# Rows loaded once, rows back from the eleventh unit, and outputs copied by ScalarE, in a fused mLSTM and feed-forward kernel

## The chip, the cores and the metric

The kernel runs on one core of a Trainium2 chip. A core has TensorE (PE, with its weight loads as a row of their own, PEld), VectorE (DVE), ScalarE (ACT), GpSimd (POOL) and SyncE (SP), which work through their own queues of instructions and wait for one another by semaphores. SP here issues nearly all DMAs, ACT the stores of the result. The metric is the device time of one execution in microseconds (us); lower is better. Everything is float32.

## The reference

Two stages. An mLSTM cell runs over 768 tokens for 4 batches of 8 heads with 40 values each; then a multiplicative feed-forward works on the 3072 x 320 rows that come out.

```
# for every batch, head and token t
m_new = max(f + m, i);  fs = exp(f + m - m_new);  is = exp(i - m_new)
C = fs * C + is * outer(v, k)         # 40 x 40
n = fs * n + is * k
h = C @ q;   denom = max(|n . q|, 1)
y[t] = sigmoid(o_gate) * h / denom
# x = y as (3072, 320)
out = ((x @ w1) * (x @ w2)) @ w3 @ w_out   # 320->1024, 1024->1024, 1024->320
```

The kernel computes the cell in chunks of 64 tokens (a score matrix within the chunk and a state carried between chunks) and multiplies w3 by w_out first, into the tile `w3o`.

## The kernel before

**Units and steps.** A unit n is 128 tokens of one batch with its 8 heads (n = chunk * 4 + batch; 24 units). One loop (from L820) runs 32 steps. Step s makes the outputs of unit s-1 and the scores and state update of unit s (`quarter_work`, L338), and between them the feed-forward of units that are done: `up`, `up_rest` for token groups 0 to 2 (four units each), and from step 19 groups 3 to 5 by a scheme of seven products (`up_by_seven`: `single`, `shared`, `left`, `product`), which needs sums of weights (`weight_sums`, POOL, steps 16 and 17) and sums of tokens (`token_sums`, DVE, steps 17, 21 and 25). `ffn_out` multiplies by `w3o`; ACT copies the result (L741) and stores it.

**Order.** TensorE's instructions are chained one behind another by `in_order`. Each engine works in the order in which the program issues to it; an instruction that waits holds up all behind it on its engine. `tc.issue_after` places a stretch of instructions behind a given one. All of SP's DMAs form one such queue.

**A unit's way.** `load` brings k, v (and q for n < 10) as rows of tokens, `load_o` the output gate, `load_u` rows of U (from n = 10; before that `rows_of_u` makes them by a DVE transpose, L295). `turn` makes kT and qT: for n < 10 by PE transposes (L95) and ACT copies (L325), from n = 10 by one DVE transpose each (L317), from rows that `load_turned` put into two halves of `gates` and `q_all`. For each of k and q and each of the two heads of a pair it issues two DMAs of 32 partitions x 640 values: one in place, one to the next 32 partitions and 32 columns to the left (so that the DVE transpose of 32 x 32 blocks finds values 32 to 39 of each token's 40 there). `weights` are eight exps on ACT (L303), `masks` two selects on POOL (L308), `weighted` and `decayed` multiplies on POOL (L330, L335).

**Outputs.** `outputs` (L419) multiplies the part that comes from the state by the gate (L423, from the bank `cell[1]` in PSUM to `h`), adds the part from the chunk in four quarters (L430, from the same bank), and then takes five operations to y: absolute value (L438), maximum and doubling (L440), reciprocal (L441), output gate (L443), product (L445). The last are spread between the scores' multiply (L397) and the state updates (L404, L414).

**y's way to x.** The feed-forward needs y transposed. For n < 15 (`NY`), `twice` doubles y's last 64 columns on POOL (L476), `x_trans` makes three PE transposes (px, L95) and one ACT copy (L486). From n = 15, `send` (issued at the top of step n+2) writes y to DRAM by four DMAs in pieces of 128 bytes (L456, L458), `get_back` (in the same step, behind the other loads) reads it by four DMAs in pieces of 384 bytes (L465), and `x_turn` is one DVE transpose (L472), which stands ahead of `turn(s + 1)` and `token_sums` on DVE. `load_turned(s + 2)` is issued at the end of a step.

**The third step.** Weights come as raw words (`fetch`), are scaled on ACT (L191) and converted on DVE (L199, L200) in `convert`. In step 2, `between` (L892) puts these, two x_trans and a `warm` between outputs and scores. `warm` issues products of the identity that nobody reads (fill, L92): there one of 128 x 512 and 38 of 64 x 64.

Of the kernel before, what the change touches and what calls it, by code (L numbers as in the profile page):

```python
# [16 lines left out]
def kernel(  # L17
# [29 lines left out]
    L = 64  # L47
# [49 lines left out]
    def warm(n, m=4, small=0):  # L97
        bank = mps([P, 4, P], "fill")
        for _ in range(n):
            mm(bank[:, 0:m], ident, ident.unsqueeze(1).to_broadcast([P, m, P]))  # L100
        for i in range(small):
            r = halves[i % 2]
            mm(bank[r, 0, 0:L], ident[r, 0:L], ident[r, 0:L])
# [8 lines left out]
    N_DIAG = 2  # L112
# [13 lines left out]
    NY = 15  # L126
    KC = KF + 1
    y_d = [dram.tile([P, 4, KC, 32], FP, name=f"y_d{n}") if n >= NY else None for n in range(NU)]
# [12 lines left out]
    def load_turned(n):  # L141
        c, b = divmod(n, B)
        for dst, src in zip(turned_in[n % 2], (k, q)):
            for hip in range(2):
                of = src[b].rearrange("(p two) s d -> two p s d", two=2)[hip, :, c * P:(c + 1) * P, :]
                for j in range(2):
                    p0, c0 = hip * DP + j * 32, (1 - j) * 32
                    nc.sync.dma_start(out=dst[p0:p0 + 32, c0:c0 + NP * RAW].rearrange("r (p e) -> r p e", p=NP),  # L148
                                      in_=of.rearrange("p (r f) d -> r p (f d)", f=4))
# [269 lines left out]
    def outputs(n, pi, ph):  # L419
        c, b = divmod(n, B)  # L420
        hs = slice(b * H, (b + 1) * H)
        h = sb.tile([P, H, D1], FP, name="h", tag="h")
        nc.vector.tensor_tensor(out=h.rearrange("p (n two) d -> p two n d", two=2), in0=pi,  # L423
                                in1=gT[:, c, hs].rearrange("p (n two) -> p two n", two=2).unsqueeze(3)
                                .to_broadcast([P, 2, NP, D1]), op=OP.mult)
        if n < N_DIAG:
            nc.vector.tensor_tensor(out=h, in0=ph, in1=h, op=OP.add)
        for x, e in quarters if n >= N_DIAG else ():
            part = h[halves[x], 0:H // 2] if x == e else h[halves[x], H // 2:H]
            nc.vector.tensor_tensor(out=part, in0=ph[x][halves[e]], in1=part, op=OP.add)  # L430

        den = sb.tile([P, H, 1], FP, name="den", tag="den")

        def steps():
            V = nc.vector
            yield V.tensor_scalar(out=den.bitcast(U32), in0=h[:, :, D:D1].bitcast(U32), scalar1=0x7FFFFFFF, scalar2=None,  # L438
                            op0=OP.bitwise_and)
            yield V.tensor_scalar(out=den, in0=den, scalar1=1.0, scalar2=2.0, op0=OP.max, op1=OP.mult)  # L440
            yield V.reciprocal(out=den, in_=den)  # L441
            e = o_t.pop(n)
            nc.vector.scalar_tensor_tensor(out=e, in0=e, scalar=1.0, in1=den.to_broadcast([P, H, D]), op0=OP.add, op1=OP.mult)  # L443
            y_t[n] = sb.tile([P, DM + REM], FP, name="y", tag="y")
            yield nc.vector.tensor_tensor(out=y_t[n][:, 0:DM].rearrange("p (h d) -> p h d", d=D), in0=h[:, :, 0:D],  # L445
                                           in1=e, op=OP.mult)

        done = steps()
        return lambda: next(done)

    def send(n):


        y = y_t.pop(n)
        for cc in range(KF):
            nc.sync.dma_start(out=y_d[n][:, :, cc, :], in_=y[:, cc * P:(cc + 1) * P].rearrange("t (i c) -> t i c", c=32))  # L456
        for i in range(0, 4, 2):
            nc.sync.dma_start(out=y_d[n][:, i:i + 2, KF, :], in_=y[:, KF * P:DM].rearrange("t (i c) -> t i c", c=32))  # L458
# [3 lines left out]
    def get_back(n):  # L462
        back_t[n] = sb.tile([P, 4, KC, 32], FP, name="yb", tag="yb", bufs=1)
        for i in range(4):
            nc.sync.dma_start(out=back_t[n][32 * i:32 * (i + 1)].rearrange("r m k c -> r m (k c)"),  # L465
                              in_=y_d[n][:, i].rearrange("(m r) k c -> r m (k c)", r=32))

    def x_turn(n):
# [3 lines left out]
        nc.vector.transpose(out=x_t[gr][:, :, j * P:(j + 1) * P].rearrange("c k (m r) -> c k m r", r=32),  # L472
# [60 lines left out]
    for i in range(NBV):  # L533
        nc.gpsimd.memset(vbuf[i][:, :, D:D1], 1.0)
# [3 lines left out]
    nc.gpsimd.memset(gates[RG:P, NP * RAW:TB], 0.0)  # L538
# [281 lines left out]
    for s in range(len(n_up)):  # L820
        if NY <= s - 2 < NU:
            send(s - 2)
# [22 lines left out]
        if s == 2 or N_DVE < s < NY + 2:  # L845
            twice(s - 2)
# [45 lines left out]
        def between():  # L892
            twice(1)
            weighted(2)
            rows_of_u(3)
            for _ in range(3):
                scale_next()
            for n in range(2):
                x_trans(n)
                if n == 0:  # L900
                    warm(1, small=38)
            for _ in range(3):
                convert()
            turn(2)
# [13 lines left out]
        with tc.issue_after(gated.ins) if gated else nullcontext():  # L918
# [11 lines left out]
            if N_DVE <= s + 1 < NU:  # L930
                gated = turn(s + 1)
# [32 lines left out]
        if s == B:  # L964
            for i, r in enumerate(third):
# [5 lines left out]
        if s >= ahead:  # L971
            while pend and len(scaled) < 2:
                scale_next()
        if N_DVE <= s + 2 < NU:
# [37 lines left out]
```

## Time and profile before

| what | value |
|---|---|
| median of 3 runs | 426.45 us (424.92, 426.45, 426.75) |
| span of the profiled execution | 425.8 us, mean granted TensorE clock 0.996 |
| TensorE busy | 414.1 us, 97% |
| VectorE, ScalarE, POOL busy | 74%, 35%, 36% |
| moved by DMA | 51.15 MB, 135211 packets |
| k and q rows of the units from 10 | 112 DMAs of 80 KB, 2.3 to 2.6 us to landing |
| y out and back | 36 DMAs of 64 or 32 KB, 36 of 48 KB |

The profiled execution's own time is its span of 425.8 us. A row of a group gives the line, the engine, the operation, output and input, shapes and count, then busy time and the mean duration in ns, then the idle time before these instructions and what ended it. A row of the timeline gives start and duration in us, then the same, with idle time and releaser in brackets. Where a releaser stands there, the engine waited for it.

### The profile page before, as it was taken

Reading aid. Unit: us, or ns where it says so; the run is one execution under the profiler, and the core shown is the slowest. Engines: PE = TensorE matmul, PEld = TensorE weight load, DVE = VectorE, ACT = ScalarE, POOL = GpSimd, SP = SyncE. Lnnn points to the kernel's source line nnn. Section 1 sums busy time; section 2 is a strip of 40 time slices with the busy share of each in tenths; the row PEclk is TensorE's granted clock in tenths of the full one; section 3 lists DMA queues with packets and bytes.
Section 4 is the critical chain, followed back from the end, with each engine's and each line's share of the span. In section 5 each row is a group of like instructions: output and inputs, shape, how many; then the busy total and the mean of one; then the engine's idle time right before and its main releaser. Section 6 shows DMA issues by size and latency. Waiting matters only on the chain.

```text
span 425.8 us, 13079 instructions
## 1 busy us (share of the span) xinstructions
PE 414.1 (97%) x5353; PEld 335.3 (79%) x5353; DVE 313.5 (74%) x635; ACT 150.1 (35%) x404; POOL 154.3 (36%) x211
## 2 busy tenths in 40 slices
PE   7989989999999999999999999999999999999996
PEld 4768878888688788787777778788778879888896
DVE  6676986888949779778736966596868699575971
ACT  4766865567723623630433313032311110210000
POOL 4421342233303303303307751546453587542100
PEclk9989999999999999999999999999999999999999
DMA  8999998598977776985425675756421120000001
GB/s 186 204 173 245 214 144 140 134 193 180 215 183 154 166 182 135 181 164 105 89 80 130 153 141 121 142 133 117 87 44 36 35 39 2 31 2 31 2 32 62
DMA packets 135211, 51.15 MB, mean 120 GB/s; under 512 B 109360, under 2 KB 126960, under 8 KB 135152
## 3 DMA queue, kind: packets, MB, share of 16 engines
q1 hardware_dynamic: 131552, 46.29, 53.9%
q10 hardware_dynamic: 3600, 4.03, 2.7%
q8 instruction: 42, 0.69, 0.7%
q14 instruction: 17, 0.14, 0.1%
HBM read 44.50 MB, written 5.80 MB: 118 GB/s over the span
## 4 chain that ended last, share of the span: by engine, by line
PE 53%; issue 20%; DVE 7%; POOL 7%; SPq 7%; DMA 5%; ACT 1%; POOLq 0%; DVEq 0%
PE cell L92 17%; PE pa L92 12%; PE o L92 8%; PE pb L92 8%; PE p L92 3%; POOL pw L308 3%; SPq L184 3%; DVE w3T L666 2%; PE pt L95 1%; POOL vw L330 1%; SPq L148 1%; DMA raw<-in_moe_w_dram 1%; PE fill L92 1%; POOL raw L659 1%; POOL state L335 1%
## 5 line engine op out<-in xcount | busy, mean ns | idle before, releaser
L335 POOL TENSOR_TENSOR state<-state,decay 128x164 f32<-128x164 f32 x40 | 20.0, 500 | 154.8 <-DVE state L404 129.0
L92 PE MATMUL pa<-xT,w 128*128 128x256 f32 x240 | 60.4, 382 | 0.0
L92 PEld LDWEIGHTS pa<-xT,w 128*128 128x128 f32 x240 | 44.4, 190 | 6.8 <-DVE h L430 0.4
L303 ACT ACTIVATE pw<-pw,aT 128x64 f32<-128x64 f32 x184 | 46.4, 339 | 3.2 <-ACT o_sb L741 1.9
L92 PE MATMUL pb<-xT,w 128*128 128x256 f32 x192 | 45.4, 379 | 0.0
L729 POOL TENSOR_TENSOR ab<-ab,a_sb 128x512 f32<-128x512 f32 x22 | 29.4, 1356 | 32.2 <-DVE ab L684 32.2
L92 PEld LDWEIGHTS pb<-xT,w 128*128 128x128 f32 x192 | 36.4, 190 | 5.0
L711 POOL TENSOR_TENSOR wo<-wo 128x512 f32<-128x512 f32 x22 | 27.4, 1268 | 29.8 <-DVE wo L686 29.8
L92 PE MATMUL pa<-xT,wr 64*64 64x256 f32 x384 | 37.0, 386 | 0.5 <-DVE wr L200 0.5
L92 PE MATMUL wp<-wo,w3T 128*128 128x320 f32 x128 | 35.9, 433 | 1.1 <-DVE ab L639 0.6
L308 POOL TENSOR_SCALAR_AFFINE_SELECT pw<-pw 64x512 f32<-64x512 f32 x48 | 35.8, 746 | 3.0 <-ACT pw L303 1.2
L92 PE MATMUL pb<-xT,wr 64*64 64x256 f32 x384 | 36.4, 380 | 0.0
L92 PE MATMUL cell<-w3o,ab 128*128 128x320 f32 x128 | 35.4, 432 | 0.0
L638 ACT ACTIVATE a_sb<-pa 128x512 f32<-128x512 f32 x24 | 14.3, 598 | 59.0 <-PE pb L92 59.0
L639 DVE TENSOR_TENSOR ab<-pb,a_sb 128x512 f32<-128x512 f32 x24 | 16.4, 688 | 23.2 <-ACT a_sb L638 22.8
L92 PEld LDWEIGHTS wp<-wo,w3T 128*128 128x128 f32 x128 | 23.8, 190 | 10.5 <-DVE ab L639 0.8
L92 PEld LDWEIGHTS cell<-w3o,ab 128*128 128x128 f32 x128 | 24.3, 190 | 9.5
L92 PEld LDWEIGHTS pa<-xT,wr 64*64 64x64 f32 x384 | 18.9, 132 | 15.4 <-issue 8.8
L686 DVE SCALAR_TENSOR_TENSOR a_sb<-pa,wo 128x512 f32<-128x512 f32 x12 | 8.3, 689 | 29.8 <-PE pa L92 29.8
L430 DVE TENSOR_TENSOR h<-cell,h 64x164 f32<-64x164 f32 x88 | 28.6, 326 | 1.6
L92 PE MATMUL po<-w3o,ab 128*128 128x320 f32 x96 | 26.4, 433 | 0.0
L92 PEld LDWEIGHTS po<-w3o,ab 128*128 128x128 f32 x96 | 18.1, 190 | 7.3
(180 smaller groups left out, 846.4 us busy)
## 6 DMA issues: line engine op xcount, KB each, us to landing
raw<-in_moe_w_dram SPq DMA_DIRECT2D x64, 128.0 KB, 3.4
kbuf<-in_k_dram SPq DMA_DIRECT2D x24, 160.0 KB, 4.5
v_all<-in_v_dram SPq DMA_DIRECT2D x24, 160.0 KB, 4.9
o_in<-in_o_gate_dram SPq DMA_DIRECT2D x24, 160.0 KB, 4.8
pw<-U_d SPq DMA_DIRECT2D x28, 128.0 KB, 3.5
raw<-in_moe_w_dram SPq DMA_DIRECT2D x5, 512.0 KB, 6.7
raw<-in_moe_w_out_dram SPq DMA_DIRECT2D x8, 320.0 KB, 4.1
gates<-in_k_dram SPq DMA_DIRECT2D x28, 80.0 KB, 2.5
```

The source lines that it names most:

```text
L92: in_order(nc.tensor.matmul(out, lhsT=lhsT, rhs=rhs, start=start, stop=stop))
L184: nc.sync.dma_start(out=dst, in_=src)
L303: nc.scalar.activation(out=pw[:, h, :], in_=src[:, h, :], func=AF.Exp, bias=aT[:, c, b * H + h:b * H + h + 1])
L308: nc.gpsimd.affine_select(out=pw[r], in_=pw[r], compare_op=OP.is_ge, fill=0.0, base=0, pattern=[[0, H], [1, L]], channel_multiplier=-1)
L335: nc.gpsimd.tensor_tensor(out=new, in0=old, op=OP.mult, in1=decay[:, b * NP:(b + 1) * NP, 2 * c + x:2 * c + x + 1] .to_broadcast([P, NP, D1]))
L430: nc.vector.tensor_tensor(out=part, in0=ph[x][halves[e]], in1=part, op=OP.add)
L638: nc.scalar.mul(out=a_sb, in_=pa, mul=UP ** -2)
L639: nc.vector.tensor_tensor(out=ab_t[gr][j][:, fs[0]:fs[-1] + 1, t0:t0 + a_sb.shape[-1]], in0=pb, in1=a_sb, op=OP.mult)
L666: nc.vector.tensor_tensor(out=dst, in0=p, in1=q, op=OP.subtract)
L686: nc.vector.scalar_tensor_tensor(out=out, in0=p, scalar=UP ** -2, in1=q, op0=OP.mult, op1=OP.add)
L711: aside_by.tensor_tensor(out=kept[j][:, 1:4:2], in0=kept[j][:, 1:3], in1=kept[j][:, 3:4].to_broadcast([128, 2, TH]), op=OP.add)
L729: aside_by.tensor_tensor(out=t[:, f:FO:FH, :], in0=t[:, f:FO:FH, :], in1=a, op=OP.mult)
```

## The change

- `load_turned` issues one DMA where it issued two, in place. The new `shift` makes the second copy on ACT: four copies of 32 partitions x 16 x 8 values per unit, ahead of `turn(s + 1)` and in ACT's queue ahead of the next unit's exps. A larger part of `gates` is set to zero by POOL in step 4.
- `NY` is 10: units 10 to 14 also go by `send`, `get_back` and `x_turn`.
- `send` is one DMA of whole rows of 384 values (1536 bytes), which include the doubled columns, so `twice` comes ahead of it for every unit; `get_back` is still four DMAs, now in pieces of 128 bytes.
- `twice(s - 1)` and `send(s - 1)` are issued at the end of step s, on SP ahead of `load_turned(s + 2)`; on POOL behind the masks of unit s+1 and in steps 16 and 17 behind `weight_sums`.
- From unit 10 (`N_OWN`), four ACT copies of 64 x 164 bring the chunk's part from PSUM to `h`, behind the multiply by the gate, and one DVE add of 128 x 328 joins the two, in place of four DVE adds.
- The way from `h` to y is four operations: reciprocal, product with -1 and maximum (its absolute value), minimum with one half and product with h, output gate. V's column of ones holds 2.0.
- In the third step, the U rows of unit 3 come behind the three converts, and the fill is two products of 128 x 512.

```diff
--- before.py
+++ after.py
@@ -94,13 +94,10 @@
     def transpose(out, in_, n=P):
         in_order(nc.tensor.transpose(out, in_, ident[0:n, 0:n]))
 
-    def warm(n, m=4, small=0):
+    def warm(n, m=4):
         bank = mps([P, 4, P], "fill")
         for _ in range(n):
             mm(bank[:, 0:m], ident, ident.unsqueeze(1).to_broadcast([P, m, P]))
-        for i in range(small):
-            r = halves[i % 2]
-            mm(bank[r, 0, 0:L], ident[r, 0:L], ident[r, 0:L])
 
     halves = [slice(0, L), slice(L, P)]
     heads = [slice(0, D), slice(DP, DP + D)]
@@ -109,7 +106,7 @@
 
     NB, NBQ, NBV = 4, 3, 5
     N_DVE = N_U = 10
-    N_DIAG = 2
+    N_DIAG, N_OWN = 2, 10
     q_all = const.tile([P, NBQ * H * DP], FP, name="q_all")
     qbuf = [q_all[:, i * H * DP:(i + 1) * H * DP].rearrange("p (h d) -> p h d", d=DP) for i in range(NBQ)]
     kbuf = [const.tile([P, H, DP], FP, name=f"kbuf{i}") for i in range(NB)]
@@ -123,9 +120,9 @@
     decay = const.tile([P, B * NP, NT], FP, name="decay")
     UT = const.tile([P, 2, 3, BH], FP, name="UT")
     U_d = dram.tile([NT, BH, L], FP, name="U_d")
-    NY = 15
+    NY = 10
     KC = KF + 1
-    y_d = [dram.tile([P, 4, KC, 32], FP, name=f"y_d{n}") if n >= NY else None for n in range(NU)]
+    y_d = [dram.tile([P, KC * P], FP, name=f"y_d{n}") if n >= NY else None for n in range(NU)]
 
     o_t, u_t = {}, {}
 
@@ -143,10 +140,15 @@
         for dst, src in zip(turned_in[n % 2], (k, q)):
             for hip in range(2):
                 of = src[b].rearrange("(p two) s d -> two p s d", two=2)[hip, :, c * P:(c + 1) * P, :]
-                for j in range(2):
-                    p0, c0 = hip * DP + j * 32, (1 - j) * 32
-                    nc.sync.dma_start(out=dst[p0:p0 + 32, c0:c0 + NP * RAW].rearrange("r (p e) -> r p e", p=NP),
-                                      in_=of.rearrange("p (r f) d -> r p (f d)", f=4))
+                nc.sync.dma_start(out=dst[hip * DP:hip * DP + 32, 32:TB].rearrange("r (p e) -> r p e", p=NP),
+                                  in_=of.rearrange("p (r f) d -> r p (f d)", f=4))
+
+    def shift(n):
+
+        for mem in turned_in[n % 2]:
+            e = mem[:, 32:TB].rearrange("r (g d) -> r g d", d=D)
+            for p0 in (0, DP):
+                nc.scalar.copy(out=e[p0 + 32:p0 + 64, :, 0:D - 32], in_=e[p0:p0 + 32, :, 32:D])
 
     def load_o(n):
         o_t[n] = io.tile([P, H, D], FP, name="o_in", tag="o_in", bufs=5)
@@ -420,12 +422,18 @@
         c, b = divmod(n, B)
         hs = slice(b * H, (b + 1) * H)
         h = sb.tile([P, H, D1], FP, name="h", tag="h")
-        nc.vector.tensor_tensor(out=h.rearrange("p (n two) d -> p two n d", two=2), in0=pi,
+        y = y_t[n] = sb.tile([P, DM + REM], FP, name="y", tag="y")
+        before = y[:, 0:H * D1].rearrange("p (h d) -> p h d", d=D1) if n >= N_OWN else h
+        nc.vector.tensor_tensor(out=before.rearrange("p (n two) d -> p two n d", two=2), in0=pi,
                                 in1=gT[:, c, hs].rearrange("p (n two) -> p two n", two=2).unsqueeze(3)
                                 .to_broadcast([P, 2, NP, D1]), op=OP.mult)
         if n < N_DIAG:
             nc.vector.tensor_tensor(out=h, in0=ph, in1=h, op=OP.add)
-        for x, e in quarters if n >= N_DIAG else ():
+        if n >= N_OWN:
+            for x, e in quarters:
+                nc.scalar.copy(out=h[halves[x], 0:H // 2] if x == e else h[halves[x], H // 2:H], in_=ph[x][halves[e]])
+            nc.vector.tensor_tensor(out=h, in0=before, in1=h, op=OP.add)
+        for x, e in quarters if N_DIAG <= n < N_OWN else ():
             part = h[halves[x], 0:H // 2] if x == e else h[halves[x], H // 2:H]
             nc.vector.tensor_tensor(out=part, in0=ph[x][halves[e]], in1=part, op=OP.add)
 
@@ -435,15 +443,12 @@
 
         def steps():
             V = nc.vector
-            yield V.tensor_scalar(out=den.bitcast(U32), in0=h[:, :, D:D1].bitcast(U32), scalar1=0x7FFFFFFF, scalar2=None,
-                            op0=OP.bitwise_and)
-            yield V.tensor_scalar(out=den, in0=den, scalar1=1.0, scalar2=2.0, op0=OP.max, op1=OP.mult)
-            yield V.reciprocal(out=den, in_=den)
-            e = o_t.pop(n)
-            nc.vector.scalar_tensor_tensor(out=e, in0=e, scalar=1.0, in1=den.to_broadcast([P, H, D]), op0=OP.add, op1=OP.mult)
-            y_t[n] = sb.tile([P, DM + REM], FP, name="y", tag="y")
-            yield nc.vector.tensor_tensor(out=y_t[n][:, 0:DM].rearrange("p (h d) -> p h d", d=D), in0=h[:, :, 0:D],
-                                           in1=e, op=OP.mult)
+            yield V.reciprocal(out=den, in_=h[:, :, D:D1])
+            yield V.scalar_tensor_tensor(out=den, in0=den, scalar=-1.0, in1=den, op0=OP.mult, op1=OP.max)
+            v = h[:, :, 0:D]
+            yield V.scalar_tensor_tensor(out=v, in0=den.to_broadcast([P, H, D]), scalar=0.5, in1=v, op0=OP.min, op1=OP.mult)
+            yield V.scalar_tensor_tensor(out=y[:, 0:DM].rearrange("p (h d) -> p h d", d=D), in0=o_t.pop(n), scalar=1.0,
+                                         in1=v, op0=OP.add, op1=OP.mult)
 
         done = steps()
         return lambda: next(done)
@@ -451,25 +456,21 @@
     def send(n):
 
 
-        y = y_t.pop(n)
-        for cc in range(KF):
-            nc.sync.dma_start(out=y_d[n][:, :, cc, :], in_=y[:, cc * P:(cc + 1) * P].rearrange("t (i c) -> t i c", c=32))
-        for i in range(0, 4, 2):
-            nc.sync.dma_start(out=y_d[n][:, i:i + 2, KF, :], in_=y[:, KF * P:DM].rearrange("t (i c) -> t i c", c=32))
+        nc.sync.dma_start(out=y_d[n], in_=y_t.pop(n))
 
     back_t = {}
 
     def get_back(n):
         back_t[n] = sb.tile([P, 4, KC, 32], FP, name="yb", tag="yb", bufs=1)
         for i in range(4):
-            nc.sync.dma_start(out=back_t[n][32 * i:32 * (i + 1)].rearrange("r m k c -> r m (k c)"),
-                              in_=y_d[n][:, i].rearrange("(m r) k c -> r m (k c)", r=32))
+            nc.sync.dma_start(out=back_t[n][32 * i:32 * (i + 1)],
+                              in_=y_d[n].rearrange("(r m) (k i c) -> i r m k c", r=32, k=KC, i=4)[i])
 
     def x_turn(n):
         gr, j = divmod(n, GT)
         if j == 0:
             x_t[gr] = ffn.tile([128, KC, TG], FP, name="xT", tag="xT")
-        nc.vector.transpose(out=x_t[gr][:, :, j * P:(j + 1) * P].rearrange("c k (m r) -> c k m r", r=32),
+        nc.vector.transpose(out=x_t[gr][:, :, j * P:(j + 1) * P].rearrange("c k (r m) -> c k m r", r=32),
                             in_=back_t.pop(n).rearrange("r m k c -> r k m c"))
 
     def twice(n):
@@ -531,11 +532,10 @@
         if i < NBQ:
             nc.gpsimd.memset(qbuf[i][:, :, D:DP], 0.0)
     for i in range(NBV):
-        nc.gpsimd.memset(vbuf[i][:, :, D:D1], 1.0)
+        nc.gpsimd.memset(vbuf[i][:, :, D:D1], 2.0)
     for t in state:
         nc.gpsimd.memset(t[0], 0.0)
     nc.gpsimd.memset(gates[:, 5 * TC:2 * TB], 0.0)
-    nc.gpsimd.memset(gates[RG:P, NP * RAW:TB], 0.0)
     nc.gpsimd.memset(pick, 0.0)
 
     nc.vector.tensor_reduce(out=pair, in_=ident[0:RG, 0:RG].rearrange("k (g j x) -> k j g x", g=GR, x=2), op=OP.add,
@@ -818,8 +818,8 @@
     turned, converted, fetched = 0, 2, 5
 
     for s in range(len(n_up)):
-        if NY <= s - 2 < NU:
-            send(s - 2)
+        if s == 2 or N_DVE < s < NY + 2:
+            twice(s - 2)
         if N_U <= s + 3 < NU:
             load_u(s + 3)
         if s < 3:
@@ -842,8 +842,6 @@
         if s < NU:
             if s >= B:
                 decayed(state[s % B][1], state[s % B][0], s, 0)
-        if s == 2 or N_DVE < s < NY + 2:
-            twice(s - 2)
         if NY <= s - 2 < NU:
             get_back(s - 2)
         while s >= N_DVE and turned < min(s - 2, NY):
@@ -892,15 +890,15 @@
         def between():
             twice(1)
             weighted(2)
-            rows_of_u(3)
             for _ in range(3):
                 scale_next()
             for n in range(2):
                 x_trans(n)
                 if n == 0:
-                    warm(1, small=38)
+                    warm(2)
             for _ in range(3):
                 convert()
+            rows_of_u(3)
             turn(2)
             block = up(*now[0])
             weighted(3)
@@ -928,6 +926,7 @@
                 if n < N_U:
                     rows_of_u(n)
             if N_DVE <= s + 1 < NU:
+                shift(s + 1)
                 gated = turn(s + 1)
             if s - 2 in range(4 * GT - 1, NU, GT):
                 token_sums((s - 2) // GT)
@@ -962,6 +961,7 @@
         if s in (16, 17):
             weight_sums(s - 16)
         if s == B:
+            nc.gpsimd.memset(gates[RG:P, 0:5 * TC], 0.0)
             for i, r in enumerate(third):
                 nc.sync.dma_start(out=U_d[i * GC:(i + 1) * GC].rearrange("c r t -> r c t"), in_=U3[r])
         with tc.issue_after(gated.ins) if N_DVE <= s + 1 < NU else nullcontext():
@@ -971,6 +971,9 @@
         if s >= ahead:
             while pend and len(scaled) < 2:
                 scale_next()
+        if NY <= s - 1 < NU:
+            twice(s - 1)
+            send(s - 1)
         if N_DVE <= s + 2 < NU:
             load_turned(s + 2)
         while todo and fetched < (n_fetch[s] if s < len(n_fetch) else converted + 4):
```

## Prediction

> **What bounds the kernel.** First the page's busy shares, then its chain, then PE's timeline for gaps.
>
> ```profile
> span 425.8 us, 13079 instructions
> PE 414.1 (97%) x5353; PEld 335.3 (79%) x5353; DVE 313.5 (74%) x635; ACT 150.1 (35%) x404; POOL 154.3 (36%) x211
> PEclk9989999999999999999999999999999999999999
> PE 53%; issue 20%; DVE 7%; POOL 7%; SPq 7%; DMA 5%; ACT 1%; POOLq 0%; DVEq 0%
> L95 PE MATMUL px<-ident,y 128*128 128x128 f32 x45 | 8.5, 295 | 1.2 <-DVE y L445 1.2
> ```
>
> TensorE is busy 97% of the span at full clock. After 30 us its gaps add up to only some 4 us. So the time moves in two ways only: an instruction leaves TensorE, or something comes too late for it. I therefore count what leaves, and then, for every part, what comes later and how much room it had.
>
> The profiled span is 425.8 us, 0.65 under the median of 426.45; I add that at the end.
>
> **y as rows for units 10 to 14.** Fifteen px transposes leave TensorE. A group of three starts 0.39 us ahead of its successor (28.41 to 28.80 below): 5 x 0.39 = 1.95 us. The last two groups lie in steps 16 and 17, whose end I find below to be set by something else, so I count 1.6 us. ScalarE loses five copies, VectorE gains five turns at 0.57 us: off the path in steps 12 to 15, 15 us long with room on both.
>
> **The third step.** The large fill plus 38 small products fill 23.59 to 28.41; now two large ones.
>
> ```profile
> 22.96 0.83 PE L95 MATMUL px<-ident,y 128*128 128x128 f32 x3 [1.19 <-DVE y L445]
> 23.59 4.90 PE L92 MATMUL fill<-ident 128*128 128x512 f32 x78
> 28.41 0.55 PE L95 MATMUL px<-ident,y 128*128 128x128 f32 x3
> 28.80 0.60 PE L95 MATMUL pt<-ident,kbuf 128*128 128x128 f32 x4
> 29.67 1.89 PE L92 MATMUL pa<-xT,w 128*128 128x256 f32 x8
> ```
>
> A large fill is two passes of 512 columns; eight passes of 256 columns take 1.73 us (29.67 to 31.40), so one fill is 0.87 and two are 1.7. From 23.35, where the first px ends (0.39 us), that gives 25.1 instead of 28.41, 3.3 us earlier; y of unit 1, which the second px needs, left VectorE at 25.6 before and has one operation less ahead of it now. Whether it stays earlier depends on the weights that follow. ScalarE's timeline shows it waiting for raw weights from DMA, and TensorE then waiting for a weight converted from them:
>
> ```profile
> 44.48 0.69 ACT L191 ACTIVATE raw<-raw 128x512 f32<-128x512 f32 x1 [0.74 <-DMA raw<-in_moe_w_dram]
> 47.33 0.43 PE L92 MATMUL pa<-xT,wr 64*64 64x256 f32 x1 [0.51 <-DVE wr L200]
> ```
>
> TensorE already waits there, at 47.33, for the end of a stream that the DMA sets. An earlier TensorE waits longer. The converts moved ahead of U's rows free raw buffers sooner, which can bring the next fetch forward, but the DMA engines are busy 8 or 9 tenths of most slices there. Bounds: 0 (all swallowed) to 3.0 us (nearly all kept). I take 0.5, the size of the wait at 47.33, which is nearest.
>
> **k and q loaded once.** 56 DMAs of 80 KB go; SP is relieved of about 2 us of issue per unit. Nothing on TensorE waited for these, so it is worth nothing by itself. ScalarE gains four copies (32x128 each) ahead of the eight exps. They cost about 4 x 0.2 = 0.8 us, estimated from 0.43 us for 320 and 0.59 for 512 elements (0.17 for 192 elements more); ScalarE is busy 35%, and in steps 11 to 17 its idle time covers it. The copies wait for the DMA, though, and the exps are queued behind them. Which brings the order.
>
> **Send, doubling and load, moved to the step's end.** Before, y of unit 15 was sent at 224.90, and the k and q rows of unit 18 had been issued at 210.93, ahead of it. Now POOL first doubles y's last columns, behind its masks and in steps 16 and 17 also behind four weight sums; then SP sends; then SP loads k and q of unit 18.
>
> ```profile
> 225.47 1.28 POOL L659 TENSOR_TENSOR raw<-w 128x512 f32<-128x512 f32 x1
> 229.28 1.28 POOL L659 TENSOR_TENSOR raw<-w,raw 128x512 f32<-128x512 f32 x1
> ```
> ```profile
> 227.54 1.14 SPq L159 DMA_DIRECT2D pw<-U_d  x2
> 231.05 3.05 SPq L465 DMA_DIRECT2D yb<-y_d  x4
> 234.20 1.80 SPq L148 DMA_DIRECT2D q_all<-in_k_dram  x4
> ```
> ```profile
> 235.87 0.58 DVE L472 STREAM_TRANSPOSE xT<-yb 128x384 f32<-128x384 f32 x1
> 236.37 1.08 DVE L317 STREAM_TRANSPOSE kT<-gates 128x512 f32<-128x512 f32 x1
> 238.22 1.12 DVE L666 TENSOR_TENSOR w3T<-xT 128x256 f32<-128x256 f32 x1
> ```
> ```profile
> 240.80 0.67 PE L92 MATMUL cell<-qT,kT 40*64 40x64 f32 x32
> 242.83 0.70 PE L92 MATMUL pa<-w3T,w 128*128 128x256 f32 x2 [0.41 <-DVE w3T L666]
> ```
>
> In the clock of the old trace: sums end 230.56; doubling (0.24) ends 230.8; one send (0.6) 231.4; four loads (half of the eight's 4.2) 233.5; then what stood at 227.54 to 231.0 (3.3 us) 236.9; the get-back's four DMAs 239.5, landing 2.0 us after the last is issued, about 241. On VectorE x's turn, the two turns of unit 18 and the four token sums stand behind that landing in this order. Turns end near 243.4 instead of 238.4, so the scores of unit 18 (240.80) stall by about 2.6. Token sums end near 246.4 instead of 242.8: the product that already waits 0.41 us starts 3.6 us late in all.
>
> The load of unit 19 is next. POOL's second sums start behind masks that are themselves later (exps of unit 18 end near 237.5, not 232.2; masks 1.8) and end near 244.7; doubling, send and loads follow to 247.6; landing near 249.6; shift copies and exps to 252. ScalarE's two copies out of the cell's bank (247.02 before, 1.1 us) end near 253.2, while the output products of step 19 (248.55, now 252.1) need that bank: another 1.0. Sum 4.6 us. Lower bound 1.5: every landing 2 us earlier than rowed here, plus the earlier start; upper 7: the get-back lands like k's 160 KB in small pieces, 4.5 us instead of 2.0. From step 20 the loads catch up, since a turn of this loop (doubling, send, load, shift, exps, masks, some 8.5 us) is shorter than a step (10.7 and more).
>
> The get-back reads pieces of 128 bytes instead of 384, the send writes 1536 instead of 128.
>
> ```profile
> yb<-y_d SPq DMA_DIRECT2D x36, 48.0 KB, 2.0
> y_d<-y SPq DMA_DIRECT2D x18, 64.0 KB, 2.3
> y_d<-y SPq DMA_DIRECT2D x18, 32.0 KB, 1.8
> ```
>
> By these rows 128-byte pieces land no slower (48 KB lies between 1.8 and 2.3), so I keep 2.0. [...]
>
> **ScalarE copies own outputs.** Four VectorE adds (1.34 us) become four copies of 64x164, at about 0.3 us (by the same two rows of 320 and 512), behind the product with the gate, and one add of about 0.4: 1.6 instead of 1.34. One step of the denominator's chain goes (0.17). Before the sevens VectorE's slack covers it. In steps 19 to 23 the scores' multiply, the state updates and the bank that the sevens' next products need all stand behind that add. The slack was about 0.2 us in the first two such steps: 0.3 us for both. From there ScalarE's work between the gate's product and the bank's release (copies, shift, exps, tanh, two copies: 5 us) has some 0.5 us of room per step; bounds 0 to 2.5 us over five steps.
>
> **Sum.** -1.6 - 0.5 + 4.6 + 0.3 = +2.8; 428.6 against the profiled 425.8; with 0.65, 429.2 us at the median, 0.65% slower. A measurement of this kernel can tell about 0.5% (2.1 us) from no change.
>
> **Rivals.**
> 1. *The stall at steps 17 to 19 isn't there* (other side). One mechanism: the get-back's landing, at 241 by my chain, comes at 238.5 or sooner, because loads and sends overlap more than I rowed. For it: the send is one DMA instead of four, and SP's issues shrink; SP's idle stretches (214.6 to 224.9) show it can wait without harm. Against: POOL's sums end at 230.56 whatever SP does. At 238.5 the turns end at 240.9 and the stall is nearly nothing; the forecast's 4.6 falls to about 0.5. Then 426.45 - 1.6 - 0.5 + 0.8 = 425.2, and with the third step's 3.0 kept, 422.7. It decides against me from a landing 2 us earlier.
> 2. *ScalarE becomes the bound in the sevens.* Copies behind a wait, then shift behind a DMA, then exps. If each of steps 19 to 23 loses 0.5 to 1 us and the get-back takes 4.5, 429.2 + 2.5 + 2.0 = 433.7. For it: the room of 0.5 us is small. Against: ACT is busy 35% over the span.
> 3. *The third step does what its fills suggest and keeps it.* 429.2 - 2.5 = 426.7, no measurable change. Against: the wait at 47.33.
>
> **How the numbers follow.** Forecast 0.47 (own range 427.5 to 431.5); stall missing 0.20; ScalarE bound 0.20; third step kept 0.13. The range reaches from rival 1's middle, 424, to rival 2's 433.7. Faster by over 0.5% (under 424.3): most of rival 1, 0.17. Within: rival 3, a rest of rival 1 and the forecast's lower third (427.5 to 428.6): 0.27. Slower: 0.56.
>
> **What would show it.** No px group after step 12; PE's second px near 24.5 and a longer wait for wr (about 4 us) near 47, if swallowed; SP's loads of unit 18 after 230 instead of 211; VectorE's turn of x waiting several us for yb's DMA in step 17; a TensorE gap of 2 to 3 us named with qT or kT, a second of about 1.5 with w3T, and one before the cell's output products with ScalarE as releaser. If no gap over 1 us lies between 225 and 260 us, the prediction is wrong there. If gaps repeat in each step from 20 on, rival 2 has it.

## The result and the profile after

The changed kernel takes 444.0 us (median of 4 runs, 441.85 to 444.87) against 426.24; the ratio is 1.0414, 95% interval 1.0383 to 1.0445. It is 4.1% slower. Executions that lie more than 1.5% above the fastest of the same kernel count in the medians given here, not in the ratios and intervals. I had forecast 0.65% slower, 429.2 us, with a range that ended at 433.7.

The page of the profiled execution, busy shares, clock and chain:

```profile
span 443.1 us, 12936 instructions
PE 416.9 (94%) x5264; PEld 334.9 (76%) x5264; DVE 295.8 (67%) x574; ACT 179.6 (41%) x511; POOL 157.2 (35%) x220
PEclk9999899999999989999999889999999999999999
PE 50%; issue 17%; SPq 8%; DVE 8%; ACT 6%; DMA 6%; POOL 4%; DVEq 0%; POOLq 0%; ACTq 0%
yb<-y_d SPq DMA_DIRECT2D x56, 48.0 KB, 3.0
```

TensorE is busy 94% instead of 97%, the clock row shows four 8s where there was none after the start, and the get-back lands 3.0 us after its issue instead of 2.0 (medians). TensorE's waits, longest first (engine, what it waited for, us in total, times, longest):

```profile
PE cell L92 <- DVE qT L319: 6.2, 1, 6.2
PE pt L95 <- issue: 2.9, 1, 2.9
PE pa L92 <- ACT xT L487: 2.8, 1, 2.8
PE cell L92 <- issue: 2.3, 1, 2.3
PE pa L92 <- DVE xT L473: 1.2, 1, 1.2
PE cell L92 <- ACT wo L702: 1.2, 3, 0.4
```

Put in order of time, by the start of each unit's score products (`cell<-qT,kT` in TensorE's timeline), after minus before:

| scores of unit | before, us | after, us | difference | what lies between |
|---|---|---|---|---|
| 2 | 34.13 | 30.90 | -3.2 | shorter fills |
| 4 | 48.93 | 50.95 | +2.0 | gap of 2.9 at 40.81, then half clock |
| 10 | 126.75 | 126.65 | -0.1 | gaps of before that are not there after |
| 12 | 158.02 | 160.32 | +2.3 | wait of 2.8 for xT from ScalarE |
| 13 | 173.31 | 179.27 | +6.0 | gap of 2.3 at 161.28, half clock |
| 14 | 188.60 | 195.70 | +7.1 | wait of 1.2 for x by rows |
| 17 | 230.12 | 236.51 | +6.4 | px products gone |
| 18 | 240.80 | 253.57 | +12.8 | wait of 6.2 for qT |
| 19 | 259.93 | 274.44 | +14.5 | half clock |
| 23 | 320.78 | 337.90 | +17.1 | 0.65 in each step |
| end | 425.8 | 443.1 | +17.3 | |

Four places lose: steps 11 to 14 (7.2 us), step 18 with what follows it (8.1), the steps from 19 on (2.8), and the start, which loses its lead of 3.2 us. The forecast had nothing lost in steps 11 to 14, 4.6 us for step 18 and what follows, 0.3 for the late steps and 0.5 of the lead kept.

**Step 18.** POOL, SP, VectorE and TensorE in order, from their timelines:

```profile
236.48 1.27 POOL L659 TENSOR_TENSOR raw<-w,raw 128x512 f32<-128x512 f32 x1
237.70 0.23 POOL L477 COPY y<-y 128x64 f32<-128x64 f32 x1
```
```profile
237.95 0.35 SPq L459 DMA_DIRECT2D y_d<-y  x1
238.40 1.38 SPq L143 DMA_DIRECT2D gates<-in_k_dram  x2
243.25 2.08 SPq L155 DMA_DIRECT2D o_in<-in_o_gate_dram  x1
245.45 3.51 SPq L466 DMA_DIRECT2D yb<-y_d  x4
```
```profile
250.84 0.86 DVE L473 STREAM_TRANSPOSE xT<-yb 128x384 f32<-128x384 f32 x1 [8.94 <-DMA yb<-y_d]
252.46 1.05 DVE L319 STREAM_TRANSPOSE qT<-gates 128x512 f32<-128x512 f32 x1
```
```profile
253.57 1.14 PE L92 MATMUL cell<-qT,kT 40*64 40x64 f32 x32 [6.20 <-DVE qT L319]
```

The doubling of unit 15 waits for POOL's fourth sum, the send for the doubling, the loads for the send, the get-back for the loads, x's turn 8.94 us for the get-back, the turn of unit 18 for x's turn, TensorE for that.

**Slow clock.** The granted clock and TensorE's busy time in stretches around that gap (the column behind PEld, DVE, ACT and POOL is the clock):

```profile
247.00:252.00 5.00, 0.38 (x28) 0.26 (x20) 1.16 (x2) 0.00 (x0) 4.92 (x6) 0.99 0.50 115
252.00:258.00 6.00, 4.43 (x71) 3.81 (x72) 4.67 (x12) 2.50 (x9) 0.07 (x1) 0.50 0.70 164
258.00:262.00 4.00, 4.00 (x19) 3.46 (x18) 1.60 (x4) 2.69 (x10) 3.27 (x6) 0.91 0.66 102
```

For almost 7 us the clock is half, and the score products of a unit take 1.14 us where they take 0.67 elsewhere. That is the step from +12.8 to +14.5.

### The profile page after: what moved, and what is told of

Same layout as the page of the kernel before. It is cut to its first block, busy times and chain, and to the rows that moved or that the text cites. A ratio compares the mean times of both kernels' runs of the same rounds, so it can differ in the third digit from the quotient of the medians.

```text
span 443.1 us, 12936 instructions
## 1 busy us (share of the span) xinstructions
PE 416.9 (94%) x5264; PEld 334.9 (76%) x5264; DVE 295.8 (67%) x574; ACT 179.6 (41%) x511; POOL 157.2 (35%) x220
## 4 chain that ended last, share of the span: by engine, by line
PE 50%; issue 17%; SPq 8%; DVE 8%; ACT 6%; DMA 6%; POOL 4%; DVEq 0%; POOLq 0%; ACTq 0%
PE cell L92 12%; PE pa L92 12%; PE o L92 8%; PE pb L92 8%; PE po L92 4%; SPq L136 4%; PE p L92 3%; PE wp L92 2%; SPq L186 2%; DMA yb<-y_d 2%; ACT pw L305 2%; DMA pw<-U_d 2%; PE pt L95 1%; SPq L155 1%; POOL pw L310 1%
## 5 line engine op out<-in xcount | busy, mean ns | idle before, releaser
L337 POOL TENSOR_TENSOR state<-state,decay 128x164 f32<-128x164 f32 x40 | 22.6, 564 | 163.7 <-DVE state L406 123.2
L92 PE MATMUL pa<-xT,w 128*128 128x256 f32 x240 | 62.8, 394 | 4.0 <-ACT xT L487 2.8
L92 PEld LDWEIGHTS pa<-xT,w 128*128 128x128 f32 x240 | 45.8, 197 | 11.6 <-ACT xT L487 3.3
L92 PE MATMUL wp<-wo,w3T 128*128 128x320 f32 x128 | 37.6, 448 | 0.7 <-DVE ab L639 0.7
L310 POOL TENSOR_SCALAR_AFFINE_SELECT pw<-pw 64x512 f32<-64x512 f32 x48 | 32.2, 671 | 13.2 <-ACT pw L305 11.7
L434 ACT COPY h<-cell 64x164 f32<-64x164 f32 x56 | 16.2, 289 | 38.9 <-DVE y L427 38.4
```

The lines of the kernel that those rows point to most:

```text
L92: in_order(nc.tensor.matmul(out, lhsT=lhsT, rhs=rhs, start=start, stop=stop))
L310: nc.gpsimd.affine_select(out=pw[r], in_=pw[r], compare_op=OP.is_ge, fill=0.0, base=0, pattern=[[0, H], [1, L]], channel_multiplier=-1)
L337: nc.gpsimd.tensor_tensor(out=new, in0=old, op=OP.mult, in1=decay[:, b * NP:(b + 1) * NP, 2 * c + x:2 * c + x + 1] .to_broadcast([P, NP, D1]))
L434: nc.scalar.copy(out=h[halves[x], 0:H // 2] if x == e else h[halves[x], H // 2:H], in_=ph[x][halves[e]])
```

## The experiments

Theory 1: ScalarE's queue is too long (copies and shift). Theory 2: the send behind the weight sums makes unit 18 late. Against both: the waits come from the DMAs themselves, or from the rows of units 10 to 14. Each edit is on the changed kernel unless it says before. Given are the median, its ratio to the kernel before and the ratio's 95% interval; waits are those of the profiled execution. In a diff, "..." stands for lines left out.

**e1, no copies by ScalarE**

```diff
-    N_DIAG, N_OWN = 2, 10
+    N_DIAG, N_OWN = 2, 24
```

> The changed kernel, but VectorE adds the four quarters of the outputs as before (no ScalarE copies of outputs). Theory 1 (ScalarE's longer queue: 1.19 us of copies behind the gate's product, and 1.26 us in which VectorE waits for them): the wait of the products for xT in step 12 falls from 2.8 to about 0.4 us, the gaps of 0.39 us (0.65 us a step) before the output products in steps 20 to 23 go, the stall of 6.2 us in step 18 stays: 444 - 2.4 - 3.0 = about 438.5. Rival (what counts is the shift behind its DMA, not the copies): gaps stay, 444.

438.69 us, ratio to before 1.0294 (1.0254 to 1.0335). The gaps before the output products are gone, and the wait for xT in step 12 is 0.52. But the total came out as expected for a partly wrong reason. The wait for x by rows in step 14 grew from 1.18 to 3.48 us, so nothing is gained in steps 11 to 14: at the scores of unit 14 the difference to the changed kernel's profile is -2.55 us, as it was at unit 4, ahead of the first unit that the edit touches. The gain that the trace gives to the edit is the 3.6 us from unit 18 to the end.

**e2, rows loaded twice, no shift**

```diff
-                nc.sync.dma_start(out=dst[hip * DP:hip * DP + 32, 32:TB].rearrange("r (p e) -> r p e", p=NP),
-                                  in_=of.rearrange("p (r f) d -> r p (f d)", f=4))
+                for j in range(2):
+                    p0, c0 = hip * DP + j * 32, (1 - j) * 32
+                    nc.sync.dma_start(out=dst[p0:p0 + 32, c0:c0 + NP * RAW].rearrange("r (p e) -> r p e", p=NP),
+                                      in_=of.rearrange("p (r f) d -> r p (f d)", f=4))
...
-                shift(s + 1)
```

> The changed kernel, but k and q rows are loaded twice by DMA as before, and ScalarE does not shift (1.25 us a unit less). Theory 1: the wait for xT in step 12 falls by 1.25 to about 1.6 us, the gaps of the steps from 20 go (-3.0), but SP issues 2 us more ahead of the get-back, so the stall of step 18 grows from 6.2 to about 8: 444 - 1.2 - 3.0 + 2 = about 442. Rival (the waits come from shifts that stand behind their DMA): the stall of step 18 falls too, 436.

443.91 us, 1.0401 (1.037 to 1.0432): no change. The wait for xT fell to 1.57 and the gaps of the late steps are gone, as theory 1 says; the stall of step 18 grew to 7.79 and the wait for x by rows to 4.10. What ScalarE saves, the longer waits behind SP's four more DMAs a unit cost. Together with e1: either of copies and shift alone fits into the late steps, both together don't.

**e3, send ahead of the weight sums**

```diff
-        if s in (16, 17):
-            weight_sums(s - 16)
...
             twice(s - 1)
             send(s - 1)
+        if s in (16, 17):
+            weight_sums(s - 16)
```

> The changed kernel, but in steps 16 and 17 the doubling and the send stand ahead of POOL's four weight sums. Theory 2 (the send behind the weight sums makes x and the turns of unit 18 late): the doubling of unit 15 comes 5 us earlier, the stall of 6.2 us in step 18 falls to about 1 and the half clock of 6.8 us behind it (3 us lost) goes: 444 - 5.2 - 2 = about 437. Rival (the get-back's small pieces and the loads ahead of it on SP set the landing): the stall stays above 4 us, 442 or more.

436.92 us, 1.0221 (1.0168 to 1.0275), 7.1 us less at the median; its four executions spread from 434.53 to 444.21. POOL's and TensorE's timelines of this run:

```profile
228.82 0.24 POOL L477 COPY y<-y 128x64 f32<-128x64 f32 x1
229.02 1.28 POOL L659 TENSOR_TENSOR raw<-w 128x512 f32<-128x512 f32 x1
```
```profile
244.50 0.69 PE L92 MATMUL cell<-qT,kT 40*64 40x64 f32 x32 [0.94 <-DVE qT L319]
```

The doubling stands ahead of the sums, the stall is 0.94 instead of 6.20, and the score products run at 0.69 us, so no half clock follows (it is 1.00 from 250 to 355 us). Theory 2 holds.

**e4, units 10 to 14 by TensorE**

```diff
-    NY = 10
+    NY = 15
```

> The changed kernel, but units 10 to 14 go by TensorE's transposes as before. Theory 1: the wait for ScalarE's copy of xT in step 12 stays (that unit is 9 in both) and another comes for the next group; the wait of 1.2 us for x by rows in step 14 goes; 15 px products come back (+1.95): about 445. Rival (the rows of units 10 to 14 are what costs the 7 us between steps 12 and 15): 437.

444.11 us, 1.0401 (1.0367 to 1.0434): no change; the rival's 437 is out. The wait for rows in step 14 is replaced by one of 2.88 us for ScalarE's copy of xT. With ScalarE's long queue x comes late either way.

**e5, e1, e2 and e3 together**

The diffs of e1, e2 and e3 in one kernel:

```diff
-    N_DIAG, N_OWN = 2, 10
+    N_DIAG, N_OWN = 2, 24
...
-                shift(s + 1)
...
+        if s in (16, 17):
+            weight_sums(s - 16)
```

> The changed kernel with three edits undone or mended at once: VectorE adds the outputs, k and q rows are loaded twice without shift, and doubling and send stand ahead of the weight sums. Left are units 10 to 14 as rows, the send of whole rows, the third step. If the three causes add up: from 436.9 (send early) the four gaps before output products go (-3) and the wait for ScalarE's xT in step 12 goes, but the wait for x by rows in step 14 grows to 3.5 or 4 us with its half clock, and SP's 2 us more leave about 3 us of stall in step 18: about 437. If instead the row wait in step 14 came from ScalarE's lateness alone, it goes too: 432.

441.76 us, 1.0363 (1.0319 to 1.0408), 5 us over what I expected. TensorE waits 7.03 us for x by rows in step 14. **e12** has the diffs of e1 and e3 alone, so rows are loaded once and shifted:

> The changed kernel with VectorE adding the outputs and the send ahead of the weight sums. Both repairs were worth 5.3 and 7.1 us alone. If they add, 444 - 12.4 = 431.6; but with the copies gone the wait for x of unit 11 by rows in step 14 stays at about 3.5 us with slow clock behind it, so that only the gaps of the last steps come off the 436.9: 433.5.

434.43 us, 1.0164 (1.0109 to 1.0219); 4.06 us of wait in step 14, 2.98 in step 18. The two repairs together are worth 9.6 us, not the sum of 12.4. Between e5 and e12 only the rows' loading differs: where the send and the get-back stand in one queue with these loads, loading once is worth 7.3 us.

**e7, the kernel before with units 12 to 14 as rows**

```diff
-    NY = 15
+    NY = 12
```

> The kernel before with units 12, 13 and 14 as rows, 10 and 11 still by TensorE. Three groups of px leave (3 x 0.39 us); these units are needed only from step 17. Theory (TensorE's queue is the bound and nothing waits for these rows): 426.3 - 1.2 = 425.1. Rival (sends and get-backs of four pieces each delay SP's other loads in steps 14 to 16): 426.5 or more.

433.83 us, 1.0186 (1.0158 to 1.0214): slower, on the rival's side, though more pieces on SP are not the main cause. SP's and ScalarE's timelines:

```profile
207.37 6.25 SPq L458 DMA_DIRECT2D y_d<-y  x2
```
```profile
210.37 0.38 ACTq L743 DMA_DIRECT2D out_dram<-o_sb  x1
```

The send's last DMA waits for the completion of that store of ScalarE's: the two share a completion semaphore, the store's last update of it comes at 213.22, and SP issues at 213.24. Of SP's 6.25 us 5.2 are that wait. Every load behind it slides (those of unit 18 start at 220.95 instead of 210.93), the send of unit 15 waits 1.7 us for another store, and step 18 stalls 6.29 us.

**e11, the same with one DMA of whole rows per send, the change's get-back, and the doubling ahead of the sums**

```diff
-    NY = 15
+    NY = 12
...
+        nc.sync.dma_start(out=y_d[n], in_=y_t.pop(n))
...
+        if NY <= s - 1 < NU:
+            twice(s - 1)
         if s in (16, 17):
             weight_sums(s - 16)
```

> The kernel before with units 12 to 14 as rows, and the change's send of whole rows and get-back in small pieces, but sent at the top of the next step as before, and doubled ahead of the weight sums. In the earlier try SP stood 6.25 us in the send of unit 14, whose DMA waited for the completion of a store of ScalarE's; one send of one DMA has that wait elsewhere. If SP's queue is all that stood against it: three px groups less, 426.3 - 1.2 = 425.1. If the row way of three units more is too long for SP even so: a stall of 2 us or more in step 18 and 429 or more.

426.81 us against 426.95 before, 0.9984 (0.9953 to 1.0016). The wait of 5.2 us in the send is gone and 1.26 us of stall are left in step 18: about what three px groups give (1.2 us) goes there. Form of the send, get-back and place of the doubling changed together, so that the send alone did it is not shown.

**The third step: e6, e8, e9, e10.** e6 is the kernel before with this part of the change alone, e9 with the order alone, e10 with the fills alone:

```diff
             weighted(2)
-            rows_of_u(3)
...
-                    warm(1, small=38)
+                    warm(2)
             for _ in range(3):
                 convert()
+            rows_of_u(3)
             turn(2)
```

> The kernel before with the third step of the change alone (U's rows behind the converts, two large fills). Theory 3 (the gain of some 3 us at 29 us is swallowed by the weights that come from DMA, and the slow clock that the fills covered falls on work): within 1 us of before, 425.3 to 427.3. Rival (kept): 423.3.

428.77 us, 1.0062 (1.0029 to 1.0094): slower by 0.6%, with an interval clear of 1.

> The kernel before with the third step, units 12 to 14 as rows and the shorter chain of the denominator (one VectorE operation less a unit). If each is worth what it takes off TensorE's queue or ahead of it: 426.3 - 1.2 - 0.5 to 1 = 424.5. If the third step is lost to a slow clock: 425.5.

e8 is e6's edit on the kernel before with two more:

```diff
-    NY = 15
+    NY = 12
...
+            yield V.reciprocal(out=den, in_=h[:, :, D:D1])
+            yield V.scalar_tensor_tensor(out=den, in0=den, scalar=-1.0, in1=den, op0=OP.mult, op1=OP.max)
```

436.12 us, 1.0242 (1.0198 to 1.0286), 2.3 us over e7, whose way of the rows it holds; the shorter chain brings nothing that shows.

The profiles of e1 to e6 and of the changed kernel had one thing in common: gaps with "issue" as their cause, behind the same matrix products counted from the program's start, the 2371st in each and the 596th in all but e1 and e2; in the kernel before they stand behind the 977th, 1608th and 2244th. A product and its weight load are two instructions: 1192, 1954, 3216, 4488 and 4742 are, modulo 256, 168, 162, 144, 136 and 134, one slowly falling line. And the page counts 42 packets of queue q8 "instruction" (0.69 MB, 16 KB each) for 2 x 5353 instructions, 41 for 2 x 5264: about one per 256. So I expected the places to move with the number of products alone:

> The kernel before with only U's rows of unit 3 behind the three converts; one large and 38 small fills stay, so TensorE's instructions are those of before, in number and order. Theory 4 (what makes the third step slower is that 74 matrix products fewer move the places where TensorE waits for nothing that the profile shows, onto stretches of short products): no such gap behind matmul 596 or 2371, those of before at matmul 977, 1608 and 2244 stay; the time is that of before, 425 to 427. Rival (the order of converts and rows costs it): 428.5.

426.24 us, 0.9983 (0.9955 to 1.0012): the same as before; its gaps stand behind products 1608 and 2244, and there is none behind 977, 596 or 2371. The order is not what costs.

> The kernel before with only the fills changed (two large, no small). Theory 4: gaps that the profile puts down to issue appear behind matmul 596 and 2371 (of 0.8 to 3 us), the products for xT wait in step 10, the gain of 2.5 to 3 us at 30 us is gone by step 10, and the time is that of the whole third step, 428.5. Rival (the order of converts and rows costs it): 426 or less.

430.56 us, 1.0075 (1.0039 to 1.0111): slower by 0.75%. So the fills alone carry the loss of the third step. TensorE's waits, and the clock in two stretches (columns: window, length, TensorE's busy time, clock, DMA share, GB/s):

```profile
PE pt L95 <- issue: 2.5, 1, 2.5
PE pa L92 <- ACT xT L486: 2.3, 1, 2.3
...
PE cell L92 <- issue: 1.5, 2, 1.2
```
```profile
40.00:43.00 3.00, 0.65 (x4) 0.62 1.18 161
43.00:47.00 4.00, 4.00 (x11) 0.50 0.86 141
119.00:122.00 3.00, 3.00 (x9) 0.54 0.81 176
```

The gaps stand behind products 596 (2.48 us at 39.88) and 2371 (1.21 us at 161.79), as written down. The other wait is DMA's. ScalarE's timeline of e10:

```profile
112.83 0.68 ACT L191 ACTIVATE raw<-raw 128x512 f32<-128x512 f32 x1 [3.87 <-DMA raw<-in_moe_w_dram]
118.27 0.45 ACT L486 COPY xT<-px 128x384 f32<-128x384 f32 x1
```

Raw weights hold up ScalarE's queue, and with it xT. TensorE's lead ends in a wait of 2.33 us, and half clock follows (0.54 from 119 to 122 us): a lead that is swallowed cost more than it was worth. How the loss divides between the gaps, this wait and the clock is not measured.

**e13 and e14**, to see whether these causes carry the whole loss, and whether the fills count in the changed kernel too. e13 is e12 with

```diff
-    NY = 10
+    NY = 12
...
-                    warm(2)
+                    warm(1, small=38)
```

> The changed kernel with four things put right at once: VectorE adds the outputs, the send stands ahead of the weight sums, units 10 and 11 go by TensorE again, and the fills are one large and 38 small. Left are rows loaded once with the shift, units 12 to 14 as rows, whole rows sent at the step's end, the shorter chain, U's rows behind the converts. If these four carry the whole loss: 426.3 - 1.2 + up to 3 us of stall left in step 18, so 425 to 428. If a part of it lies elsewhere (shift, single load): 431 or more.

426.32 us against 425.90 before, 1.0012 (0.9972 to 1.0052): back at the time before, with the rows loaded once, the shift, the whole rows and the shorter chain in it. Its longest wait for another engine after 50 us is 0.71 (step 18). Four edits are undone at once: together they carry the whole loss. Two of them, the way of units 10 and 11 and the fills, are the 8.1 us from e12 to here, and no run parts these.

> The changed kernel with the fills of before (one large, 38 small), nothing else undone. If the fills cost in the changed kernel what they cost alone (2.5 to 4.3 us), 444 - 3 = 441, and no gap put down to issue behind matmul 596 and 2371. If their loss is hidden there behind the later waits: 444.

441.75 us, 1.0384 (1.0314 to 1.0455): neither of the two gaps, and 2.3 us less at the median than with the new fills; but the intervals overlap, so that no gain is shown.

No kernel here beats the one before by more than the runs can tell.

## Why the prediction was wrong

**Right.** The direction (slower) and the chain of step 18 link by link. That the lead at 29 us would not last was right by luck: the wait for a converted weight near 47 us, which was to swallow it, did not come; a gap of 2.92 us that nothing in the program causes, at 40.81, and the half clock behind it did. Px products cost 0.39 us a group: from unit 14 to 17 the difference falls by 0.7 us while two of the five groups go. The four weight sums (232.66 to 237.70) put the doubling off by 5.0 us; e3 shows what that was worth by moving it.

**Failed: "Sum 4.6 us" for steps 17 to 19.** It measured 8.1 (6.4 by the scores of unit 18, 1.7 to those of unit 19). Inside, the landing at "about 241" was the mis-sized term: with the 6.4 us that the kernel was late, 250.8 answers to 244.4. Of these 3.4 us, POOL's sums ending late gave 0.8, the loads between those of k and q and the get-back 1.2 (the output gate's 2.08 against 1.02), the get-back's four DMAs 0.9 (3.51 instead of the 2.6 that I took), and the rest lies mostly in the landing: 2.5 us from the last issue, at 248.35, to x's turn. For the landing I had kept 2.0 us by the rows of the send's 128-byte pieces; the median over all get-backs of the changed kernel is 3.0. The row I chose was of writes to DRAM, the get-back reads. The two stalls that I put behind the first, of 1.0 each, did not come: the four token sums took 1.5 us (253.36 to 254.90) instead of 4.6 before (238.22 to 242.77). Before, POOL's second sums ran beside them, to 241.89; now these had ended at 251.47. Half clock took their place.

**Failed: "0.3 us for both" and "its idle time covers it" for ScalarE.** I priced the copies rightly (1.19 us for four) and the shift at 0.8 (1.25), but held each against ScalarE's idle time by itself. VectorE waits 1.26 us for the copies, and copies, shift, exps, tanh and two bank copies make one chain in each late step; it ends 0.39 us late and costs 0.65 a step (VectorE's wait: engine, what it waited for, us in total, times, longest). That was rival 2's mechanism.

```profile
DVE h L435 <- ACT h L434: 17.6, 14, 1.3
```

In steps 11 to 14 I looked for no queue behind ScalarE at all: the copy of xT stands behind all this and the scaling of raw weights. ScalarE's timeline of the changed kernel:

```profile
143.03 1.19 ACT L434 COPY h<-cell 64x164 f32<-64x164 f32 x4 [1.16 <-DVE y L427]
144.24 1.25 ACT L151 COPY gates<-gates 32x128 f32<-32x128 f32 x4
145.52 2.02 ACT L305 ACTIVATE pw<-pw,aT 128x64 f32<-128x64 f32 x8
150.03 0.45 ACT L487 COPY xT<-px 128x384 f32<-128x384 f32 x1
```

TensorE wants xT at 147.7. A mean share of 35% said nothing of this step.

**Half right: the single load "worth nothing by itself".** With all else as in the change it is (e2, 443.9 against 444.0), because shift and DMAs cost the same there; beside e12 it is worth 7.3 us (e5), because SP's queue had become part of the path.

**Failed: "off the path in steps 12 to 15" for units 10 and 11.** Their x is needed by the products of step 14, and the get-back of unit 11 stands on SP behind eight fetches of raw weights (3.69 us) and five loads:

```profile
170.76 3.69 SPq L186 DMA_DIRECT2D raw<-in_moe_w_dram  x8
178.31 3.01 SPq L466 DMA_DIRECT2D yb<-y_d  x4
```
```profile
184.26 0.76 DVE L450 SCALAR_TENSOR_TENSOR y<-o_in,h 128x320 f32<-128x320 f32 x1
184.94 0.85 DVE L473 STREAM_TRANSPOSE xT<-yb 128x384 f32<-128x384 f32 x1
```

In the changed kernel the rows landed at 183.88, and x's turn came at 184.94 without a wait for them: it stood behind VectorE's own chain, which had waited 1.26 us for ScalarE's copies before 181.64. The DMA sets the time once the copies are gone: x's turn waits 2.66 us for it in e1 and 3.23 in e12. Units 12 to 14 could go without harm (e11, e13), at no gain that shows.

**Failed: "I take 0.5" for the third step.** It is a loss, of 2.7 and 3.6 us at the median beside the kernel before (e6, e10); in the changed kernel 2.3 (e14), which is not clear of noise. The bounds that I gave, 0 to 3.0 of gain, held no loss: I asked where the lead would end and not what ending it costs.

**Not in the sum at all: the clock.** The kernel before has its half clock under the fills at the start (0.57 from 23 to 26 us); after the change it falls on work after three of the four waits of over 2 us, at some 1.7 us (half) per stretch of 3.4. The profile has it around 44 and 163 us, and for a double stretch from 252 us; the wait at 147.72 had none behind it (1.00 from 148 to 160 us). I priced every wait at its length alone.

## What to carry to other kernels

Before work goes to an engine with a low mean share, list what stands behind it in that engine's queue in the very step where its result is wanted, and add the moved pieces up: two that fit alone (copies of 1.19 us, a shift of 1.25) did not fit together. When a send is tied to a helper's operation, look at what that helper does just before, and at what the same DMA queue carries behind it. A TensorE that is 97% busy should not be made early in front of data that arrive at a fixed time: what it gained in e10 it waited off (2.33 us for xT), and it paid the slow clock (0.54 behind that wait) on top.

## What was not expected of the hardware

- **A wait that nothing in the program causes.** In the profiles of before and after TensorE stands 0.30 to 2.92 us at the five places named above, whose counts of instructions lie on one slowly falling line modulo 256, each time within or just behind a row of short products: behind 27 of 32 products in the changed kernel's step 12 (2.30 us), behind 20 of 32 in an early step of the kernel before (1.49). The changed kernel's timeline:

```profile
160.81 0.47 PE L92 MATMUL cell<-vw,kbuf 64*40 64x41 f32 x27
163.58 0.37 PE L92 MATMUL cell<-vw,kbuf 64*40 64x41 f32 x5 [2.30 <-issue]
```

e9 and e10 show that 74 products fewer move these places. That they are the 16 KB packets of queue q8 is argued from the counts, and the packets' own times speak for it: the gaps at these five places end 1.4 to 1.7 us after a packet of q8 has ended (here the packet took 160.80 to 162.19, at the first gap, of 40.81 to 43.73, 40.75 to 41.98).

- **Half clock after gaps.** In the profiles of before and after and behind two waits of e10 the clock fell to 0.50 four times for 3.4 us and twice for 6.8. In the changed kernel gaps of 2.30 us (at 161.28), 2.92 (at 40.81) and 6.20 (up to 253.57) were followed by it, in e10 one of 2.48 (at 39.88) and one of 2.33 (up to 118.78); one of 2.82 (at 147.72) was not. So no length of a gap that decides it is shown. A gap cost its length alone or, by my estimate from half of 3.4, 1.7 us and more on top, which may be why single executions of one kernel differ by several us (441.85 to 444.87 here, at mean clocks of 0.992 and 0.984).
- **Stores of one engine held up loads of another.** SP waited 5.2 us in e7 for a store that ScalarE had issued, through a completion semaphore that both use. SP waits for such stores in the kernel before too, four times in its get-backs and for up to 4.8 us; there no wait of TensorE is for x by rows.
